# Reordered low parts on VectorE and GpSimd, and two weight loads moved from the first attention pairs to pairs 5 and 6

## The chip, the cores and the metric

The kernel runs on one core of a Trainium2 chip. The metric is the device time of one execution in microseconds; the time before is the median of three runs.

## The reference, cut to what matters

Causal attention over 2 batches of 12 heads (448 rows, head size 64), then a gated layer, then a second layer with a softmax-weighted unit and a layer norm:

```python
scores = scale * q @ k.T; masked; attn = exp(scores - max) / (sum + 1e-9)
x = (attn @ v), heads side by side            # 896 x 768
g = sigmoid(x @ w_gate) * (x @ w_val)         # 896 x 1536
x = g @ w_out                                 # 896 x 768
h = x @ w_in                                  # 896 x 1024
solu = h * softmax(h); ln = layer_norm(solu) * g_ln
out = ln @ w_out2                             # 896 x 768
```

All of it is float32. Every float32 operand of a product is split into a high part (rounded to the tensor engine's fast float32 form) and a low part (the rest), and a product is three products: high by high, high by low, low by high.

## The kernel before, in words

Attention works on 12 pairs of heads. Its order is written out by hand: a list `STEPS` of entries (offset, engine, function, first pair, last pair), in which entry (o, e, f) issues `f(p)` at step `s = 8 * p + o` on engine `e`. A pair has 8 steps. At each step the main loop goes through the engines (E tensor engine, A ScalarE, D VectorE, S the SyncE queue, P GpSimd), and within one engine through the list from top to bottom, so that the list's order decides between entries of one step. Each engine works its instructions off in the order in which they were issued. "Pair 7" below is the stretch in which the tensor engine starts with the score products of pair 7.

For a pair p the work is:

- `load_qk(p)` and `load_v(p)`, loads on SyncE's queue into two raw buffers each, so that a load for p + 2 must be issued after the last reading of p's buffer.
- `prep_k_hi`, `prep_q_hi`, `prep_v_hi` (L225, L236): the high parts, on GpSimd. `prep_k_lo` (L231, tile `qks`) and `prep_v_lo` (L231, tile `v`, two instructions): the low parts, on GpSimd; `prep_q_lo` (L252): q's low part, on VectorE. `prep_k_lo` also issues the load of q and k for p + 2, `prep_v_lo` that of v.
- `sc_mm`: masks (L352) and score products (L365) in two groups of tiles, (3, 0) and (2, 1). In a tile the third of three terms reads q's low part. `sc_max` (L380): row maxima on VectorE. `sc_exp` (L392): exponentials with their row sums, on ScalarE.
- `sums` (L396, GpSimd), `recips` (L400 and L401, VectorE): the reciprocals of the row sums. `rs_rows` (L406) writes them to DRAM in four small transfers, and `rs_bcast` (L412) reads them back spread over the partitions, after the small ones have landed.
- `tr_mm` (L435): transposes of the exponentials, in four units 0 to 3 that share two PSUM buffers. `tr_hi` (L442, ScalarE) copies a unit out as its high part, `tr_lo` (L231, VectorE, tile `pt`) takes its low part and so frees the buffer: unit 2 needs the low part of unit 0, unit 3 that of unit 1.
- `pv_mm` (L466): the product with v, in eight pieces. `x_mul` (L472, VectorE): the product by the reciprocals. `x_hi` (L223, ScalarE) and `x_lo` (L231, GpSimd, tile `xy`): the split of x.

In the order before, VectorE does in pair p: maxima of tiles 3 and 0, low part of unit 3 of pair p - 2, `prep_q_lo(p + 1)`, `recips(p - 1)`, maxima of tile 2, low part of unit 0 of pair p - 1, maxima of tile 1, low part of unit 1, `x_mul(p - 2)`, low part of unit 2. GpSimd does: `sums(p - 1)`, `prep_v_lo(p - 1)`, `x_lo(p - 3)`, `prep_k_lo(p + 1)`, `prep_k_hi(p + 2)`, `prep_q_hi(p + 2)`, `prep_v_hi(p)`.

The weights of the gated layer come as raw 64-bit words in chunks of 128 x 1536 words of 4 bytes, into two raw buffers. `dma_next()` issues the next load. In attention two are issued at fixed steps (8 and 12, both among the steps of pair 1); `bits_steps` turns a chunk into float32 from step 88 on, on ScalarE and VectorE, and issues the load that follows. A first part of the gated layer (`early_tiles`, L498) runs on the tensor engine behind step 96.

Of the kernel before, what the change touches and what calls it, by code (L numbers as in the profile page):

```python
# [19 lines left out]
B, H, S, D = 2, 12, 448, 64  # L20
# [18 lines left out]
def f32(ap):  # L39
    return ap.bitcast(F32)  # L40
# [3 lines left out]
def attn_moe_moe2(ctx: ExitStack, tc: tile.TileContext, qk, v, w_gv, w_out, w_in2, w_out2, g_ln, out):  # L44
# [50 lines left out]
    def dma_next():  # L95
        if pos["dma"] < len(order):
            it = order[pos["dma"]]
            a, n = src[it]
            raw = ring.tile([128, 2 * CH], I32, tag="raw", name="raw")
            nc.sync.dma_start(out=raw[:, :2 * n], in_=a.bitcast(I32))  # L100
            raw_t[it] = raw
            pos["dma"] += 1

    def bits_steps(it):


        assert order[pos["bits"]] == it
        pos["bits"] += 1
        n = src[it][1]
        w = raw_t.pop(it)[:, :2 * n].rearrange("p (n t) -> p n t", t=2)  # L110
        w0, w1 = w[:, :, 0], w[:, :, 1]
        nc.scalar.activation(out=w1.bitcast(F32), in_=w1.bitcast(F32), func=AF.Copy, scale=2.0 ** -112)  # L112
        yield
        tt = ring.tile([128, CH], I32, tag="t", name="t")[:, :n]
        nc.vector.tensor_scalar(out=tt, in0=w1, scalar1=3, scalar2=None, op0=ALU.logical_shift_left)  # L115
        yield
        nc.vector.scalar_tensor_tensor(out=tt, in0=w1, scalar=-2 ** 31, in1=tt,  # L117
                                       op0=ALU.bitwise_and, op1=ALU.bitwise_or)
        yield
        nc.vector.scalar_tensor_tensor(out=tt, in0=w0, scalar=29, in1=tt,  # L120
                                       op0=ALU.logical_shift_right, op1=ALU.bitwise_or)
        t_t[it] = tt.bitcast(F32)
        dma_next()
        yield
# [11 lines left out]
    def chunk_hi(c):  # L136
        if c < NCH and c not in hl_t:
            hl_t[c] = ring.tile([128, 2, CH], FR, tag="hl", name="hl")
            w_hi(c, hl_t[c][:, 0])

    def chunk_lo(c):
        if c in t_t:
            w_lo(c, hl_t[c][:, 0], hl_t[c][:, 1])
# [50 lines left out]
    with ExitStack() as actx:  # L194
# [14 lines left out]
        def load_qk(p):  # L209
            if p < NH // 2:  # L210
                r = qkr.tile([128, 2, S], F32, tag="qkr", name="qkr")
                both = qk[2 * p:2 * p + 2].rearrange("a d i s -> (a d) i s")
                for i in (1, 0) if p == 0 else (slice(0, 2),):
                    nc.sync.dma_start(out=r[:, i], in_=both[:, i])
                qk_raw[p] = r
# [14 lines left out]
        def sub(eng, out, a, b):  # L230
            (nc.gpsimd if eng == 'P' else nc.vector).tensor_tensor(out=out, in0=a, in1=b, op=ALU.subtract)  # L231
# [12 lines left out]

        def prep_k_lo(p):
            sub('P' if p else 'D', qk_sp[p][:, 3], qk_raw[p][:, 1], f32(qk_sp[p][:, 0]))
            if p:
                load_qk(p + 2)

        def prep_q_lo(p):  # L250
            t = qk_sp[p]
            nc.vector.scalar_tensor_tensor(out=t[:, 2], in0=qk_raw[p][:, 0], scalar=0.125, in1=f32(t[:, 1]),  # L252
                                           op0=ALU.mult, op1=ALU.subtract)

        def v_parts(p):
            return (v_raw[p % 2][:, 0:3].rearrange("p j (a d) -> p j a d", a=2),
                    *(v2[p % 2][:, i].rearrange("p j (a d) -> p j a d", a=3)[:, :, 0:3:2] for i in range(2)))
# [65 lines left out]
        prep_k_hi(0, 'D')  # L323
        prep_q_hi(0, 'A')
        prep_k_lo(0)
        prep_q_lo(0)
        load_qk(2)
        load_v(0)
# [49 lines left out]
        def sc_max(p, *tiles):  # L378
            for i in tiles:
                nc.vector.reduce_max(out=sum_t[p % 3][:, 8 + 2 * i:10 + 2 * i], in_=ps_both[p, i], axis=AX.X,  # L380
                                     negate=True)
# [47 lines left out]
        def tr_width(u):  # L429
            return 512 if u else S  # L430
# [13 lines left out]
        def tr_lo(p, u):  # L444
            w = tr_width(u)
            sub('D', pt_t[p][:, 1, u, :w], ps_tr.pop((p, u))[:, :w], f32(pt_t[p][:, 0, u, :w]))
# [39 lines left out]
        def early_tiles():  # L486
# [19 lines left out]
        NPR = NH // 2  # L506
# [13 lines left out]
            (14, 'A', lambda p: tr_hi(p, 2)), (6, 'A', lambda p: sc_exp(p, (1,)), 1),  # L520
            (-1, 'D', lambda p: sc_max(p, 3, 0), 2, 3),
            (0, 'D', lambda p: sc_max(p, 3, 0), 3), (16, 'D', lambda p: tr_lo(p, 3)),
            (-7, 'D', prep_q_lo, 3), (9, 'D', recips),
            (2, 'D', lambda p: sc_max(p, 2), 2), (11, 'D', lambda p: tr_lo(p, 0), 1), (3, 'D', lambda p: sc_max(p, 1), 2),
            (13, 'D', lambda p: tr_lo(p, 1)), (21, 'D', x_mul), (15, 'D', lambda p: tr_lo(p, 2)),
            (8, 'P', sums, 1), (9, 'P', prep_v_lo, 1), (25, 'P', x_lo, 0, NPR - 1), (23, 'P', x_lo, NPR - 1),
            (9, 'S', rs_rows), (9, 'S', rs_bcast),
            (-10, 'P', prep_k_hi, 3), (-9, 'P', prep_q_hi, 3), (-4, 'P', prep_k_lo, 3), (7, 'P', prep_v_hi, 1),
        )

        sc_mm(0, (0, 1))
        keep_warm(ps[:, 0], 6)
        prep_k_hi(1)
        prep_q_hi(1, 'A')
        prep_q_lo(1)
        prep_k_lo(1)
        for e in range(2):
            sc_max_of(0, e, 3, 0)
# [26 lines left out]
        def steps(s, eng):  # L565
            for s0, e, f, *ps in STEPS:
                p, r = divmod(s - s0, PER)
                lo, hi = (*ps, NPR)[:2] if ps else (0, NPR)
                if e == eng and r == 0 and max(lo, 1 if s0 < 0 else 0) <= p < hi:
                    f(p)  # L570


        for s in range(PER * NPR + 26):
            steps(s, 'E')
            for _ in range(2):
                if s >= PER * NPR and left and next(early):
                    left -= 1
            steps(s, 'A')
            steps(s, 'D')
            steps(s, 'S')  # L580
            steps(s, 'P')
            if s in (8, 12):
                dma_next()

            for c in range(2 * NE + 2):
                e = s - 88 - 8 * c
                if e in (3, 5, 7):
                    next(bits_now)
                if e == 8 and c < 2 * NE:
                    chunk_hi(c)  # L590
                if e == 9 and c < 2 * NE:
                    chunk_lo(c)
                if e == 0:
                    bits_now = bits_steps(c)
                    next(bits_now)
# [237 lines left out]
```

## Time and profile before

| what | value |
|---|---|
| median of three runs | 496.69 us (496.26 to 498.13) |
| the profiled execution | 497.59 us, span 495.8 us |
| tensor engine busy | 481.9 us (97%) |
| VectorE busy | 329.7 us (67%) |
| ScalarE busy | 221.8 us (45%) |
| GpSimd busy | 120.8 us (24%) |
| tensor engine clock | granted in full throughout |

A span runs from the first to the last instruction; the profiled execution's own time is 1.79 us longer. Shares of busy time are averages over stages: attention takes the first quarter, and there all five engines are busy most of the time. The trace names an instruction by its line, its engine, and the tile that it writes and reads; in brackets stand the idle time of its engine before it and what ended it. "x4" is four instructions shown as one row.

### The profile page before, as it was taken

How to read it: one execution, taken by the hardware profiler on the slowest of the kernel's cores; microseconds unless marked ns; L12 is line 12 of the kernel's file. 1: busy time of each engine (PE TensorE's matmuls, PEld its weight loads, DVE VectorE, ACT ScalarE, POOL GpSimd, SP SyncE). 2: the span in 40 equal slices, each digit the busy share in tenths (PEclk: the TensorE clock that was granted, in tenths of full speed). 3: DMA queues.
4: the chain of work that ended last, by engine and by line, in shares of the span. 5: the costliest groups of instructions: out<-in, count | busy, mean ns of one | idle time of the engine just before them, and what ended most of it. 6: DMA issues, size and time to landing. Idle time of an engine off the chain costs nothing.

```text
span 495.8 us, 7596 instructions
## 1 busy us (share of the span) xinstructions
PE 481.9 (97%) x2907; PEld 440.8 (89%) x2907; DVE 329.7 (67%) x508; ACT 221.8 (45%) x471; POOL 120.8 (24%) x190
## 2 busy tenths in 40 slices
PE   8979988999999999999999999999999999999997
PEld 7868878899999999999999999999988888899996
DVE  7788888887556788777779647777635887821110
ACT  6868787955334434534543423433421433323111
POOL 5749878530000000000000000000060778610000
PEclk9999999999999999999999999999999999999999
DMA  5454433243322535433444333533431221001001
GB/s 192 138 156 148 155 93 104 61 147 127 129 76 94 169 131 167 153 117 116 167 159 139 127 108 127 167 128 116 163 128 26 103 69 60 0 33 62 34 32 65
DMA packets 15685, 55.60 MB, mean 112 GB/s; under 512 B 2720, under 2 KB 4768, under 8 KB 15648
## 3 DMA queue, kind: packets, MB, share of 16 engines
q1 hardware_dynamic: 15648, 55.11, 33.1%
q8 instruction: 23, 0.38, 0.3%
q14 instruction: 14, 0.11, 0.1%
HBM read 52.30 MB, written 2.80 MB: 111 GB/s over the span
## 4 chain that ended last, share of the span: by engine, by line
PE 84%; DVE 7%; DMA 4%; issue 2%; ACT 1%; SPq 1%; DVEq 0%; ACTq 0%
PE gv L639 34%; PE pm L669 18%; PE po L762 12%; PE h L701 12%; DVE pt L231 2%; PE x L466 2%; DVE sum L380 2%; PE t L435 2%; PE gv L498 2%; DVE qks L252 2%; PE s L365 1%; DMA rd<-rs32q 1%; DMA rb<-rd 1%; PE tp L744 1%; DMA qkr<-in_qk_dram 1%
## 5 line engine op out<-in xcount | busy, mean ns | idle before, releaser
L639 PE MATMUL gv<-xy,hl 128*128 128x448 f32 x828 | 168.1, 365 | 0.0
L639 PEld LDWEIGHTS gv<-xy,hl 128*128 128x128 f32 x828 | 155.4, 188 | 12.3
L669 PE MATMUL pm<-g,hl 128*128 128x448 f32 x432 | 87.7, 365 | 0.0
L669 PEld LDWEIGHTS pm<-g,hl 128*128 128x128 f32 x432 | 81.1, 188 | 6.4
L686 POOL TENSOR_SCALAR t<-t,g_sb 128x768 f32<-128x768 f32 x8 | 9.0, 1124 | 247.7 <-PE pm L669 247.7
L134 DVE TENSOR_TENSOR hl<-t,hl 128x768 fp32r<-128x768 f32 x36 | 35.1, 975 | 40.8 <-ACT hl L131 39.1
L762 PE MATMUL po<-wo,lt 128*128 128x384 f32 x336 | 60.7, 340 | 0.0
L701 PE MATMUL h<-wi,xy 128*128 128x512 f32 x252 | 59.3, 396 | 0.0
L762 PEld LDWEIGHTS po<-wo,lt 128*128 128x128 f32 x336 | 58.7, 188 | 0.2 <-POOL wo L691 0.2
L701 PEld LDWEIGHTS h<-wi,xy 128*128 128x128 f32 x252 | 47.1, 187 | 11.4
L117 DVE SCALAR_TENSOR_TENSOR t<-raw,t 128x768 int32<-128x768 int32 (+1 forms) x56 | 52.6, 939 | 1.8
L120 DVE SCALAR_TENSOR_TENSOR t<-raw,t 128x768 int32<-128x768 int32 (+1 forms) x56 | 52.0, 929 | 1.7
L112 ACT ACTIVATE raw<-raw 128x768 f32<-128x768 f32 (+1 forms) x56 | 48.2, 867 | 9.2 <-DMA raw<-in_wo_dram 5.9
L466 PE MATMUL x<-pt,v 128*128 128x384 f32 (+3 forms) x252 | 51.0, 324 | 0.0
L392 ACT ACTIVATE p<-s,sum 128x320 f32<-128x320 f32 (+3 forms) x92 | 43.7, 494 | 14.4 <-DVE sum L380 11.1
L466 PEld LDWEIGHTS x<-pt,v 128*128 128x128 f32 x252 | 37.0, 190 | 1.6
L231 DVE TENSOR_TENSOR pt<-t,pt 128x512 fp32r<-128x512 f32 (+1 forms) x48 | 32.0, 666 | 4.7 <-ACT pt L442 4.6
L171 DVE TENSOR_TENSOR lt<-tp,lt 128x512 fp32r<-128x512 f32 x14 | 9.7, 690 | 36.4 <-ACT lt L170 36.4
L435 PE MATMUL t<-ident,p 128*128 128x128 f32 x180 | 28.0, 276 | 5.6 <-DVE pt L231 5.6
L115 DVE TENSOR_SCALAR t<-raw 128x768 int32<-128x768 int32 (+1 forms) x56 | 30.6, 546 | 2.7 <-ACT raw L112 2.7
L380 DVE TENSOR_REDUCE sum<-s 128x2 f32<-128x640 f32 (+3 forms) x44 | 28.8, 677 | 5.1 <-PE s L365 5.1
L131 ACT CAST hl<-t 128x768 fp32r<-128x768 f32 x36 | 30.0, 834 | 4.6 <-PE pm L669 4.2
(97 smaller groups left out, 481.6 us busy)
## 6 DMA issues: line engine op xcount, KB each, us to landing
raw<-in_gv_dram SPq DMA_DIRECT2D x24, 768.0 KB
raw<-in_wo_dram SPq DMA_DIRECT2D x20, 768.0 KB
raw<-in_wi_dram SPq DMA_DIRECT2D x12, 512.0 KB
qkr<-in_qk_dram SPq DMA_DIRECT2D x11, 448.0 KB
vr<-in_v_dram SPq DMA_DIRECT2D x12, 256.0 KB
rb<-rd SPq DMA_DIRECT2D x24, 112.0 KB
out_dram<-o SPq DMA_DIRECT2D x6, 384.0 KB
rd<-rs32q SPq DMA_DIRECT2D x48, 1.0 KB
```

Source lines behind the costliest of these rows:

```text
L112: nc.scalar.activation(out=w1.bitcast(F32), in_=w1.bitcast(F32), func=AF.Copy, scale=2.0 ** -112)
L117: nc.vector.scalar_tensor_tensor(out=tt, in0=w1, scalar=-2 ** 31, in1=tt, op0=ALU.bitwise_and, op1=ALU.bitwise_or)
L120: nc.vector.scalar_tensor_tensor(out=tt, in0=w0, scalar=29, in1=tt, op0=ALU.logical_shift_right, op1=ALU.bitwise_or)
L231: (nc.gpsimd if eng == 'P' else nc.vector).tensor_tensor(out=out, in0=a, in1=b, op=ALU.subtract)
L380: nc.vector.reduce_max(out=sum_t[p % 3][:, 8 + 2 * i:10 + 2 * i], in_=ps_both[p, i], axis=AX.X, negate=True)
L392: nc.scalar.activation(out=p_t[p % 2][:, POFF[i] + (1 - e) * n:POFF[i] + (2 - e) * n], in_=ps_sc[p, i][1 - e], func=AF.Exp, bias=mx, scale ...
L435: nc.tensor.transpose(ps[:, max(c, 0):max(c, 0) + 128], p_t[p % 2][:, k:k + 128], ident if c >= 0 else identx)
L466: nc.tensor.matmul(out=ps[:, q0:], lhsT=l, rhs=pt_t[pr][:, c, u, c0:c0 + S - q0], start=(chunk == 0 and n == 0), stop=(chunk == 7 and n == ...
L639: nc.tensor.matmul(out=ps[i, b], lhsT=w[:, a, cs], rhs=xy[kk][:, x, b * S:(b + 1) * S], start=(kk == 0 and a == 0 and x == 0), stop=(kk == ...
L669: nc.tensor.matmul(out=ps[b], lhsT=w[:, a, cs], rhs=g_t[kk][:, x, b * S:(b + 1) * S], start=(kk == 0 and a == 0 and x == 0), stop=(kk == N ...
L701: nc.tensor.matmul(out=h[:, n * 512:(n + 1) * 512], lhsT=xy[kk][:, a, tk], rhs=wi[n * NK + kk][:, c], start=(kk == 0 and i == 0), stop=(kk ...
L762: nc.tensor.matmul(out=ps[n], lhsT=lts[k // 4][:, a, k % 4], rhs=wo[k][:, c, cs], start=(k == 0 and i == 0), stop=(k == NF2 - 1 and i == 2))
```

## The change

In VectorE's list `recips` (9) now stands first, then the low part of unit 0 (offset 11 becomes 10), then the maxima of tiles 2 and 1. `prep_q_lo` goes from offset -7 to -2, behind `x_mul` (21, which falls on an earlier step of the pair) and ahead of the low part of unit 2 in the pair's order. `prep_v_lo` goes from offset 9 to 8 and stands ahead of `sums`. For pairs from 3 on, the load of q and k for p + 2 is issued by `prep_q_lo`, which is now the last reader of the raw buffer, and not by `prep_k_lo`. The two first weight loads are issued at steps 44 and 52.

```diff
         def prep_k_lo(p):
             sub('P' if p else 'D', qk_sp[p][:, 3], qk_raw[p][:, 1], f32(qk_sp[p][:, 0]))
-            if p:
+            if 0 < p < 3:
                 load_qk(p + 2)
 
         def prep_q_lo(p):
             t = qk_sp[p]
             nc.vector.scalar_tensor_tensor(out=t[:, 2], in0=qk_raw[p][:, 0], scalar=0.125, in1=f32(t[:, 1]),
                                            op0=ALU.mult, op1=ALU.subtract)
+            if p > 2:
+                load_qk(p + 2)
...
-            (-7, 'D', prep_q_lo, 3), (9, 'D', recips),
-            (2, 'D', lambda p: sc_max(p, 2), 2), (11, 'D', lambda p: tr_lo(p, 0), 1), (3, 'D', lambda p: sc_max(p, 1), 2),
-            (13, 'D', lambda p: tr_lo(p, 1)), (21, 'D', x_mul), (15, 'D', lambda p: tr_lo(p, 2)),
-            (8, 'P', sums, 1), (9, 'P', prep_v_lo, 1), (25, 'P', x_lo, 0, NPR - 1), (23, 'P', x_lo, NPR - 1),
+            (9, 'D', recips), (10, 'D', lambda p: tr_lo(p, 0), 1),
+            (2, 'D', lambda p: sc_max(p, 2), 2), (3, 'D', lambda p: sc_max(p, 1), 2),
+            (13, 'D', lambda p: tr_lo(p, 1)), (21, 'D', x_mul), (-2, 'D', prep_q_lo, 3), (15, 'D', lambda p: tr_lo(p, 2)),
+            (8, 'P', prep_v_lo, 1), (8, 'P', sums, 1), (25, 'P', x_lo, 0, NPR - 1), (23, 'P', x_lo, NPR - 1),
...
-            if s in (8, 12):
+            if s in (44, 52):
                 dma_next()
```

## Rows read from the trace of the kernel before

**Rows 1.** Stretches by pair (3, 4, 7, 11): length; busy time of each engine, clock, DMA.

```profile
23.16:33.81 10.65, 7.67 (x76) 6.62 (x76) 7.35 (x14) 6.17 (x22) 3.90 (x5) 1.00 0.58 178
33.81:41.29 7.48, 7.29 (x76) 6.62 (x75) 6.26 (x13) 6.20 (x22) 6.07 (x9) 1.00 0.42 134
57.21:65.16 7.95, 7.29 (x76) 6.62 (x76) 6.73 (x13) 6.21 (x22) 6.12 (x9) 1.00 0.36 123
...
88.97:97.28 8.31, 7.61 (x79) 6.99 (x78) 7.63 (x15) 8.09 (x28) 4.29 (x8) 1.00 0.28 86
```

**Rows 2.** Waits of PE, pairs 5 to 10: total us, times, longest.

```profile
PE t L435 <- DVE pt L231: 3.9, 6, 0.7
```

**Rows 3.** Instructions in order of time, pair 7: start, us, engine, line, tiles.

```profile
57.31 1.10 PE L365 MATMUL s<-qks 64*128 64x448 f32 x12
...
57.99 0.25 POOL L396 TENSOR_SCALAR rs8i<-sum 128x8 f32<-128x8 f32 x1 [1.62 <-ACT p L392]
...
58.32 1.42 POOL L231 TENSOR_TENSOR v<-vr,v 128x384 fp32r<-128x384 f32 x2
...
59.70 1.16 POOL L231 TENSOR_TENSOR xy<-xf,xy 128x448 fp32r<-128x448 f32 x1
...
60.26 1.08 DVE L252 SCALAR_TENSOR_TENSOR qks<-qkr,qks 128x448 fp32r<-128x448 f32 x1
...
60.49 0.53 ACT L442 CAST pt<-t 128x448 fp32r<-128x448 f32 x1
...
61.27 0.19 DVE L400 RECIPROCAL rs32t<-rs8i 128x8 f32<-128x8 f32 x1
...
61.63 0.78 DVE L380 TENSOR_REDUCE sum<-s 128x2 f32<-128x640 f32 x1
...
62.10 0.61 ACT L442 CAST pt<-t 128x512 fp32r<-128x512 f32 x1
62.33 0.62 DVE L231 TENSOR_TENSOR pt<-t,pt 128x448 fp32r<-128x448 f32 x1
62.51 0.56 POOL L225 TENSOR_SCALAR qks<-qkr 128x448 fp32r<-128x448 f32 x1
...
63.00 0.66 PE L435 MATMUL t<-ident,p 128*128 128x128 f32 x4 [0.66 <-DVE pt L231]
...
63.32 0.68 DVE L231 TENSOR_TENSOR pt<-t,pt 128x512 fp32r<-128x512 f32 x1
...
63.56 0.77 POOL L225 TENSOR_SCALAR v<-vr 128x384 fp32r<-128x384 f32 x2
...
64.28 0.60 PE L435 MATMUL t<-ident,p 128*128 128x128 f32 x4
...
65.08 0.69 DVE L231 TENSOR_TENSOR pt<-t,pt 128x512 fp32r<-128x512 f32 x1 [0.54 <-ACT pt L442]
```

**Rows 4.** Instructions in order of time, from pair 2 to pair 3.

```profile
14.17 0.42 SPq L100 DMA_DIRECT2D raw<-in_gv_dram  x1
...
25.97 0.62 DVE L472 TENSOR_TENSOR xf<-x,rb 128x448 f32<-128x448 f32 x1 [4.17 <-DMA rb<-rd]
```

**Rows 5.** Chain that ended last, to 135 us: start, length, what.

```profile
15.92 5.36 DMA rd<-rs32q
...
86.53 1.17 DMA rd<-rs32q
```

**Rows 6.** Instructions in order of time, pair 11 and the first one behind it.

```profile
93.95 0.60 PE L435 MATMUL t<-ident,p 128*128 128x128 f32 x4
...
97.28 0.33 PE L435 MATMUL t<-identx,p 128*128 128x128 f32 x1 [0.71 <-DVE pt L231]
```

**Rows 7.** Instructions on the split q and k: shortest, median, longest in ns.

```profile
L252 DVE SCALAR_TENSOR_TENSOR qks<-qkr,qks x12: 617/1075/1222, 4.6 to 84.1; 128x448 fp32r<-128x448 f32 x12
```

**Rows 8.** Instructions in order of time, pair 9: a load and its reader.

```profile
73.82 0.38 SPq L214 DMA_DIRECT2D qkr<-in_qk_dram  x1
...
79.16 0.57 POOL L225 TENSOR_SCALAR qks<-qkr 128x448 fp32r<-128x448 f32 x1 [0.93 <-DMA qkr<-in_qk_dram]
```

## The prediction

> **What bounds the kernel now.** I read the stretches first, one per head pair of the attention stage, then who waited for whom on the tensor engine, then one pair in order of time, then the two places where pairs differ. The tensor engine's clock is granted in full in every stretch shown [rows 1], so times differ by waits alone. From pair 5 to pair 10 a pair takes 7.95 us, of which the tensor engine is busy 7.29; pair 4 takes 7.48 and pair 3 takes 10.65 with 7.67 busy [rows 1]. (A pair's stretch runs from its masks to the next pair's; the row of pair 7, 57.21 to 65.16, stands for six between 7.93 and 7.97.) After attention the tensor engine runs without such waits, so what attention saves should reach the end.
>
> In pairs 5 to 10 the engine has one kind of wait: six times the transposes of line 435 wait for a low part of line 231, 3.9 us together [rows 2]. The reader is to follow one of them backwards [rows 3]. The transposes of unit 2 at 63.00 stood 0.66 us still, until the vector engine had finished the low part of unit 0 (62.33 + 0.62 = 62.95), which frees their PSUM buffer. That low part needed only ScalarE's copy of unit 0, over at 60.49 + 0.53 = 61.02. It started 1.3 us later because q's low part (60.26, 1.08 us), the reciprocals (61.27) and the third tile's maxima (61.63) stand ahead of it in VectorE's order. So the bound is the order on VectorE.
>
> Pair 3 has another cause [rows 4, 5]. The first weight load is issued at 14.17, just ahead of the four small transfers of the first pair's reciprocals. Those land 5.36 us after the last is issued, where the same transfers take 1.17 us late in the stage [rows 5]. The broadcast, the product that reads it, and all that is queued behind the product on VectorE follow: the product waits 4.17 us, until 25.97 [rows 4]; over pair 3 the tensor engine is idle 10.65 - 7.67 = 2.98 us [rows 1].
>
> **The change, part by part. First, the order on VectorE (pairs 5 to 10).** Taking q's low part out lets the reciprocals start at 60.26; they and the transpose take 61.63 - 61.27 = 0.36, so VectorE is free at 60.62. The low part of unit 0, now next, waits for ScalarE until 61.02, runs from about 61.05 to 61.67, and unit 2's transposes, ready at 63.00 - 0.66 = 62.34, no longer wait [rows 3]. The maxima start at 61.67 rather than 61.63, so nothing is late there. The low part of unit 1 comes 0.70 (61.63 to 62.33, the maxima) and 0.99 (62.33 to 63.32) after 61.05, at 62.74; ScalarE's copy of unit 1 is over at 62.71; it ends at 63.42. Unit 3's transposes, then due at 64.28 - 0.66 = 63.62, have 0.2 us to spare: that edge is next.
>
> What a pair saves is bounded from below by the wait itself, 3.9 us over six pairs [rows 2], and from above by pair 11, which has no q part to prepare and the old order otherwise: there unit 2's transposes start 93.95 - 88.97 = 4.98 us into the pair, against 63.00 - 57.21 = 5.79, which is 0.81 [rows 1, 3, 6]. Six pairs: 3.9 to 4.9. I take 0.75 each, nearer to pair 11, since that is this very pipeline without the wait: **4.5 us**. A pair is then 7.2 us.
>
> q's low part itself goes behind the product, where VectorE stood idle 0.54 us before 65.08, waiting for ScalarE [rows 3]. By the shift above (63.32 to 62.74) the product is over at 65.08 - 0.54 - 0.58 = 63.96; q's low part runs to 64.58 at its shortest form (0.62) or 65.04 at its usual (1.08) [rows 7]. The next pair starts at 64.41 and its third term, which reads it, comes about half way through the twelve dots of 1.10 us that start 0.10 into a pair [rows 3]: about 65.0. Covered, with 0 to 0.4 us; I cost it at nothing, and if the cover is gone it is rival 1.
>
> **Second, v's low part ahead of the sums.** GpSimd stood idle 1.62 us ahead of the sums, waiting for ScalarE's exponentials [rows 3]. v's high part is over at 63.56 + 0.77 = 64.33; the low part of 1.42 us fits to 65.75, before the 57.99 + 7.95 = 65.94 at which the next sums ran before. With the shorter pair the sums may come some 0.4 us late, but the reciprocals that wait for them are due 3.05 us into the pair (60.26 - 57.21), at 67.46: 1.4 us of cover. Cost nothing. Behind the reciprocals on VectorE are the low part of unit 0, the maxima and so the tensor engine; a late sums would stall all of it.
>
> **Third, the loads of q and k behind q's low part.** The load of two pairs ahead is now issued at about 64.6 to 65.05, 7.4 to 7.8 into a pair; on SP's queue it stays behind the reciprocal transfers but now goes ahead of v's load. The slowest landing seen took 79.16 - 73.82 = 5.3 us [rows 8], so it lands by 12.7 to 13.1, that is 5.5 to 5.9 into the next pair. From there GpSimd needs 1.05 (62.51 to 63.56), 0.77, 1.42 and 0.25 for both high parts, v and the sums, 3.5 together [rows 3, 7]: 9.0 to 9.4, against reciprocals due at 7.2 + 3.05 = 10.25. Cost nothing, 0.8 us to spare.
>
> **Fourth, the two weight loads.** In pair 3 the delay of 5.36 - 1.17 = 4.19 us was made by all that was in flight: by their shapes 768 KB of weights, 448 of q and k, 256 of v. By size, the weights' share is 4.19 x 768/1472 = 2.2 us. The small transfers then land at about 19, and the broadcast before or about 21.8 (25.97 - 4.17), when the product is due; a rest of a microsecond on VectorE is harmless, since of 4.17 us only 2.98 reached the tensor engine. Pair 3 saves at least its idle time, 2.98, and at most 10.65 - 7.2 = 3.45 if it runs like the rest: **3.2 us**. Pair 4: 7.48 - 7.2, **0.3 us**.
>
> In pairs 5 and 6 the loads come back on SP's queue ahead of the load of q and k for pairs 8 and 9, which lands 2.2 us later: 7.7 to 8.1, and the sums at 11.2 to 11.6 instead of the due 10.25. Of this 1.0 to 1.4 us, 0.4 is the time in which the low part of unit 0 waits for ScalarE anyway, and 0.6 is unit 2's spare time (62.34 against 61.67). So nothing at a quicker landing, and up to 1.0 us for each load, the second of which starts from a later queue. I take 0.35 each: **-0.7 us** (0 to -2.0). The weights themselves are first used in pair 11, so their own lateness costs nothing.
>
> **Fifth, pair 11 and the end.** There q's low part was absent already, so the new order only adds VectorE's 0.4 us wait for ScalarE's copy (60.62 to 61.02 in the same place of pair 7), and VectorE sets the pace: the transposes at 97.28 waited 0.71 us for it [rows 6]. Also v's low part now meets other instructions of the weights' preparation. **-0.5 us** (0 to -1.3, that is 0.4 and two delays of 1.08 - 0.62).
>
> Sum: 4.5 + 3.2 + 0.3 - 0.7 - 0.5 = 6.8 us. The profiled execution took 497.59 us (span 495.8 and 1.79 around it), so it would be 490.8; it was 0.90 above the median of 496.69, which becomes **489.9 us**.
>
> **Rivals.** *1. q's low part meets v's low part on the way.* Now q's low part begins at 60.26 while GpSimd's x part runs to 59.70 + 1.16 = 60.86, and it ends at 61.34, 0.48 behind that; alone it takes 0.62 [rows 3, 7]. In the new order v's low part follows v's high part directly and lies in the very place of q's low part. If it is locked out until the first of v's two instructions is over (three quarters of the 1.42 by their columns, so 64.33 + 1.07) it ends 0.48 behind that, at 65.9, 0.9 after the third term is due; since either may come first I count half, 0.4 in each pair: 6 x 0.4 = 2.4 off, 492.3 us. For it: the places agree to half a microsecond. Against: GpSimd also gets rid of its collision now, and a late q part has its own spare time. Chance 0.14. The Trainium skill's "SBUF — State Buffer" (Who interferes with whom) has this as a rule: a VectorE instruction with two SBUF inputs and a GpSimd instruction that reads SBUF exclude each other, and the later one to issue is blocked until the first is over. By that rule, which the 0.48 us bears out, the sum is 6.8 where the two miss each other and 4.4 where they meet.
>
> *2. The loads in pairs 5 and 6 disturb more than their own pair:* late q and k carry GpSimd's lateness through pairs 7 to 9, 3.5 us instead of 0.7: 492.7 us. For: pair 3 shows what a load ahead of small transfers does. Against: a pair has a spare microsecond or more on GpSimd. Chance 0.10.
>
> *3. The first stall stays:* the small transfers wait behind q, k and v instead, and pair 3 saves 1.0 and not 3.2: 492.1 us. For: 704 of 1472 KB remain in flight. Against: the weights are the larger half, and the product has 1.2 us of lateness (4.17 - 2.98) that never reached the tensor engine. Chance 0.08.
>
> *4. Slower: the sums, behind v's low part, behind a late load, hold the reciprocals in every pair.* To be 3 us slower, 9.8 us have to be lost over pairs 3 to 10, 1.2 each, and 0.4 us of slack first: the reciprocals 1.6 late, which with 0.8 to spare takes a landing of 5.3 + 0.8 + 1.6 = 7.7 us after issue in each pair. That gives 499.7 us. For: the load is issued behind a later instruction and everything hangs on one queue. Against: the slowest landing seen is 5.3 us. Chance 0.04.
>
> **How the numbers follow.** The forecast has 0.60, with its own range of 488.4 to 491.6 (savings of 8.3 to 5.1, the bounds not all at one end); the rivals 0.36; 0.04 is left for several together that cancel the gain. The range reaches down to 488.0 and up to 492.9, which takes in rivals 1 to 3. A change of 0.5%, 2.5 us, is about what a measurement of this kernel can tell from none: faster than 494.2 is the forecast and the rivals 1 to 3, 0.92; the same 0.04; slower 0.04.
>
> **What would show it.** Right: no idle time ahead of unit 2's transposes in pairs 5 to 10; a pair of about 7.2 us; the product of pair 0 without its 4.17 us wait; pair 3 below 7.8 us. Unit 0's low part starts straight after ScalarE's copy. Wrong: dots waiting for q's low part (rival 1); GpSimd waiting over 2 us for q and k in pairs 6 and 7, and reciprocals waiting for the sums (2, 4); a product that still waits for its broadcast (3); unit 3's transposes waiting for unit 1's low part, the edge with 0.2 us.

## The result, and the profile after

The changed kernel takes 491.68 us (median of 8 runs, 490.61 to 495.26) against 496.70 us before (8 runs): a ratio of 0.9906, 95% interval 0.9879 to 0.9933. The profiled execution took 492.44 us with a span of 490.7 us, 5.1 us under the span before. The forecast was 489.9 us, the range 488.0 to 492.9.

The stretches by pair of the changed kernel, for pairs 3, 6, 7, 8 and 11, with the columns of [rows 1] (length; busy PE, PEld, DVE, ACT, POOL; clock; DMA share; GB/s):

```profile
23.02:30.24 7.22, 7.22 (x76) 6.52 (x75) 6.50 (x13) 5.38 (x19) 3.30 (x5) 1.00 0.40 133
...
44.76:51.99 7.23, 7.23 (x76) 6.52 (x75) 6.43 (x13) 6.19 (x23) 4.75 (x7) 1.00 0.69 241
51.99:59.88 7.89, 7.51 (x76) 6.55 (x75) 6.35 (x13) 6.19 (x23) 5.74 (x9) 1.00 0.63 187
59.88:68.94 9.06, 7.52 (x76) 6.54 (x77) 6.37 (x13) 6.21 (x23) 7.17 (x12) 1.00 0.43 140
...
83.42:92.19 8.77, 7.63 (x79) 6.93 (x79) 8.14 (x16) 8.53 (x29) 5.69 (x8) 1.00 0.18 56
```

Pair 3 went from 10.65 to 7.22 us, and quiet pairs (5, 6, 9 and 10, in which nothing waits for a late transfer) from 7.95 to 7.24: in them the tensor engine is busy for the whole stretch. Pairs 7 and 8 are the exceptions. The two weight loads stand at steps of pairs 5 and 6, but the queue comes to them at 45.36 and 54.66, in the stretches of pairs 6 and 7 (0.69 of the DMA engines' time in pair 6): the loss shows one pair behind each. Pair 11 grew from 8.31 to 8.77.

How a quiet pair now runs is seen on VectorE and on the tensor engine's weight loads (PEld), in order of time, for the places that answer to [rows 3] and [rows 4]:

```profile
22.15 0.62 DVE L474 TENSOR_TENSOR xf<-x,rb 128x448 f32<-128x448 f32 x1 [0.67 <-DMA rb<-rd]
...
48.58 0.62 DVE L231 TENSOR_TENSOR pt<-t,pt 128x448 fp32r<-128x448 f32 x1 [0.34 <-ACT pt L444]
49.12 1.28 DVE L382 TENSOR_REDUCE sum<-s 128x2 f32<-128x640 f32 x2
...
50.32 0.68 DVE L231 TENSOR_TENSOR pt<-t,pt 128x512 fp32r<-128x512 f32 x1
...
51.05 0.42 PEld L437 LDWEIGHTS t<-ident,p 128*128 128x128 f32 x4 [0.29 <-DVE pt L231]
...
51.45 0.62 DVE L252 SCALAR_TENSOR_TENSOR qks<-qkr,qks 128x448 fp32r<-128x448 f32 x1
52.07 0.69 DVE L231 TENSOR_TENSOR pt<-t,pt 128x512 fp32r<-128x512 f32 x1
```

The product of pair 0 waits 0.67 us for its broadcast and not 4.17. The low part of unit 0 waits 0.34 us for ScalarE's copy and then starts, as forecast; q's low part fills the gap ahead of unit 2's low part and takes its shortest form. Unit 1's low part is over at 51.00, and the weight loads of unit 3's transposes had already waited 0.29 us for it: that edge has nothing to spare, though the matmuls in flight cover the wait.

What goes wrong in pairs 7 and 8 is one chain over four engines. In order of time, with the SyncE queue as SPq:

```profile
45.36 1.20 SPq L100 DMA_DIRECT2D raw<-in_gv_dram  x1
46.67 0.36 SPq L214 DMA_DIRECT2D qkr<-in_qk_dram  x1
...
48.27 1.30 SPq L408 DMA_DIRECT2D rd<-rs32q  x4
...
52.55 0.56 POOL L225 TENSOR_SCALAR qks<-qkr 128x448 fp32r<-128x448 f32 x1 [2.87 <-DMA qkr<-in_qk_dram]
53.43 1.19 SPq L414 DMA_DIRECT2D rb<-rd  x2
54.66 0.59 SPq L100 DMA_DIRECT2D raw<-in_gv_dram  x1
55.36 0.36 SPq L214 DMA_DIRECT2D qkr<-in_qk_dram  x1
...
55.86 0.26 POOL L398 TENSOR_SCALAR rs8i<-sum 128x8 f32<-128x8 f32 x1
56.15 0.20 DVE L402 RECIPROCAL rs32t<-rs8i 128x8 f32<-128x8 f32 x1 [1.01 <-POOL rs8i L398]
...
58.95 0.66 PE L437 MATMUL t<-ident,p 128*128 128x128 f32 x4 [0.35 <-DVE pt L231]
...
61.60 0.57 POOL L225 TENSOR_SCALAR qks<-qkr 128x448 fp32r<-128x448 f32 x1 [3.15 <-DMA qkr<-in_qk_dram]
...
65.19 0.20 DVE L402 RECIPROCAL rs32t<-rs8i 128x8 f32<-128x8 f32 x1 [2.17 <-POOL rs8i L398]
...
66.20 0.66 PE L437 MATMUL t<-ident,p 128*128 128x128 f32 x4 [1.19 <-DVE pt L231]
```

The weights stand ahead of q and k on the queue; the first instruction that reads q or k starts 5.9 us after their issue (46.67 to 52.55), GpSimd stands still 2.87 us and comes late to v and the sums; the reciprocals wait 1.01 us for the sums, and the transposes for the low parts behind the reciprocals. The second time is worse, for the broadcast of the pair before had to wait for its small transfers (48.27 to 53.43), which kept the second weight load and all that follows it back on the queue.

### The profile page after: what moved, and what is told of

Same layout as the page of the kernel before. It is cut to its first block, busy times and chain, and to the rows that moved or that the text cites. A ratio compares the mean times of both kernels' runs of the same rounds, so it can differ in the third digit from the quotient of the medians.

```text
span 490.7 us, 7583 instructions
## 1 busy us (share of the span) xinstructions
PE 481.4 (98%) x2907; PEld 439.8 (90%) x2907; DVE 327.5 (67%) x508; ACT 221.2 (45%) x471; POOL 119.9 (24%) x190
## 4 chain that ended last, share of the span: by engine, by line
PE 90%; DVE 4%; ACT 3%; DMA 2%; issue 0%; SPq 0%; POOL 0%; ACTq 0%
PE gv L641 34%; PE pm L671 18%; PE po L764 12%; PE h L703 12%; PE x L468 5%; PE t L437 3%; PE s L367 3%; DVE sum L382 2%; PE gv L500 2%; ACT p L394 2%; PE tp L746 1%; DVE pt L231 1%; DMA qkr<-in_qk_dram 1%; PE s L354 0%; DMA rb<-rd 0%
## 5 line engine op out<-in xcount | busy, mean ns | idle before, releaser
L183 ACT ACTIVATE wk<-gv 128x448 f32<-128x448 f32 x23 | 11.3, 542 | 44.3 <-PE gv L641 44.3
```

## The experiments

The first seven are profiles of one execution each; numbers 8 to 11 were also timed over several runs. The length of a pair is the distance between the first masks of two pairs in each trace; pair 11 is counted to the first transposes behind it.

| kernel | span | pairs 3 to 10, us | pair 11 |
|---|---|---|---|
| before | 495.8 | 10.65 7.48 7.97 7.95 7.95 7.94 7.93 7.94 | 8.31 |
| changed | 490.7 | 7.22 7.28 7.24 7.23 7.89 9.06 7.23 7.25 | 8.77 |
| 1 weights late | 488.7 | 7.24 7.24 7.26 7.23 7.73 7.27 7.25 7.39 | 8.78 |
| 2 weights behind q and k | 489.9 | 7.25 7.23 7.25 7.25 7.34 7.23 7.97 7.75 | 9.10 |
| 3 weights early | 495.0 | 13.35 7.25 7.23 7.44 7.47 7.23 7.49 7.24 | 8.76 |
| 4 sums first | 490.1 | 7.24 7.26 7.27 7.24 7.24 8.17 7.25 7.26 | 8.77 |
| 5 weights alone | 493.4 | 7.82 7.94 7.96 7.94 7.94 7.49 8.85 7.49 | 8.31 |
| 6 maxima first | 489.4 | 7.21 7.52 7.20 7.63 7.21 7.94 7.21 7.22 | 8.78 |
| 7 q early | 496.4 | 8.24 8.27 8.26 8.28 8.26 8.26 8.29 8.26 | 8.77 |
| 8 late, and pair 11 | 489.1 | 7.25 7.55 7.26 7.40 7.50 7.25 7.24 7.24 | 8.74 |
| 9 sums first, late | 487.8 | 7.24 7.26 7.24 7.24 7.23 7.24 7.25 7.25 | 8.30 |
| 10 q and weights alone | 487.6 | 7.21 7.22 7.23 7.20 7.21 7.22 7.22 7.20 | 8.32 |
| 11 changed again | 490.1 | 7.24 7.72 7.25 7.23 7.25 8.73 7.26 7.25 | 8.77 |

**1. The weight loads behind all loads of q and k.**

```diff
-            if s in (44, 52):
+            if s in (74, 82):
```

> The two first weight loads go to steps 74 and 82, behind the last load of q and k (step 70) and ahead of their first use at step 88; all else as changed. Theory (the weight loads stand ahead of the loads of q and k on SyncE's queue and make them, GpSimd, the sums and the reciprocals late): pairs 7 and 8 fall from 7.89 and 9.06 us to about 7.24 each, the reciprocals no longer wait for the sums there, the span falls from 490.7 to about 488.3. Rival (the load of q and k is late because it is now issued behind q's low part, whatever stands ahead of it): pairs 7 and 8 stay near 7.9 and 9.1, span 490.7.

The span fell to 488.7 us, pair 8 to 7.27, and the reciprocals wait for the sums nowhere. The theory holds for the weights, but pair 7 stayed at 7.73 (and pair 10 at 7.39, with q's low part at 1.12 us), and for another reason. GpSimd, VectorE and the tensor engine in order of time:

```profile
51.24 1.80 POOL L231 TENSOR_TENSOR v<-vr,v 128x384 fp32r<-128x384 f32 x2
51.29 1.44 DVE L252 SCALAR_TENSOR_TENSOR qks<-qkr,qks 128x448 fp32r<-128x448 f32 x1
...
52.79 0.73 PE L367 MATMUL s<-qks 64*128 64x448 f32 x8 [0.21 <-DVE qks L252]
```

v's low part began 0.05 us ahead of q's low part, which took 1.44 us instead of 0.62, and the score products waited for it. This is rival 1. At that place in the changed kernel's profile the two did not meet: while q's low part ran (51.45 to 52.07), GpSimd stood still for q and k.

**2. The same weight loads two steps later, behind the load of q and k of the same pair.**

```diff
-            if s in (44, 52):
+            if s in (46, 54):
```

> The two weight loads stay in pairs 5 and 6 but two steps later (46 and 54), so that they stand behind the load of q and k of the same pair on SyncE's queue; the same bytes in the same pairs. Theory (order on the queue): q and k land on time, pairs 7 and 8 at 7.24 to 7.5, span 488.3 to 489. Rival (bytes: any 768 KB more in these pairs make the transfers late): pairs 7 and 8 stay over 7.8 and over 8.8, span 490.5.

Pairs 7 and 8 were nearly quiet (7.34 and 7.23), as the order on the queue would have it. Yet pairs 9 and 10 took 7.97 and 7.75, which neither side had expected; and the span, 489.9, lies outside the theory's 488.3 to 489. The queue and VectorE in order of time:

```profile
48.30 1.30 SPq L408 DMA_DIRECT2D rd<-rs32q  x4
52.38 1.09 SPq L414 DMA_DIRECT2D rb<-rd  x2
...
55.64 1.31 SPq L408 DMA_DIRECT2D rd<-rs32q  x4
61.53 1.09 SPq L414 DMA_DIRECT2D rb<-rd  x2
62.73 0.53 SPq L214 DMA_DIRECT2D qkr<-in_qk_dram  x1
...
70.83 0.20 DVE L402 RECIPROCAL rs32t<-rs8i 128x8 f32<-128x8 f32 x1 [1.09 <-POOL rs8i L398]
```

The weights no longer stand ahead of the load of q and k, but still, as in the changed kernel, ahead of the small transfers. The broadcast is issued 4.1 and 5.9 us after them, against 2.3 to 3.7 in undisturbed pairs of the changed kernel (41.10 to 44.23, for one), and the next load of q and k stands behind the broadcast; the reciprocals then wait for the sums, 1.09 us in pair 9 and 0.87 in pair 10. So the bytes do disturb, two pairs later than in the changed kernel, by way of the queue's wait.

**3. The weight loads at their old steps, with the reorderings.**

```diff
-            if s in (44, 52):
+            if s in (8, 12):
```

> The weight loads back at steps 8 and 12; the three reorderings stay. Theory: the product of pair 0 waits about 4 us for its broadcast again, pair 3 takes 10 to 10.6 us, pairs 7 and 8 7.24 each: span 490.7 - 2.46 + 3 = 491.2. Rival (the reordering, not the weight loads, took the stall out of pair 3): pair 3 stays at 7.2, span 488.3.

The stall of pair 3 is back and larger than before the change: 13.35 us. The span, 495.0, is 3.8 us above what was expected. VectorE and the tensor engine in order of time:

```profile
25.80 0.62 DVE L474 TENSOR_TENSOR xf<-x,rb 128x448 f32<-128x448 f32 x1 [4.28 <-DMA rb<-rd]
26.34 0.61 DVE L252 SCALAR_TENSOR_TENSOR qks<-qkr,qks 128x448 fp32r<-128x448 f32 x1
...
27.01 1.22 PE L367 MATMUL s<-qks 64*128 64x448 f32 x8 [3.21 <-DVE qks L252]
```

The product waits as in [rows 4], but now q's low part is queued behind it, and the score products of pair 3 wait 3.21 us for that. That is about half of the 6.1 us by which the pair exceeds a quiet one. The rest is the tensor engine's clock, in the stretch behind the wait (columns as in [rows 1]):

```profile
27.01:32.70 5.69, 5.69 (x40) 5.48 (x40) 3.07 (x7) 1.62 (x5) 2.23 (x2) 0.50 0.44 145
```

The granted clock is the lower of the two levels there (0.50, 1.2 GHz) and full again from 33.30; the engine is busy throughout, and 5.69 us at half the clock are an estimated 2.8 us lost. In the kernel before the longest wait in pair 3 was 1.45 us, and the clock stayed full [rows 1]. Behind the product, q's low part has no cover for a product that waits: without the move of the weights the reorderings save 0.8 us of span in all, in this one execution. Pairs 6, 7 and 9 took 7.44 to 7.49, behind q parts of 1.18 to 1.20 us, as in experiment 1.

**4. The sums ahead of v's low part again.**

```diff
-            (8, 'P', prep_v_lo, 1), (8, 'P', sums, 1),
+            (8, 'P', sums, 1), (8, 'P', prep_v_lo, 1),
```

> The sums ahead of v's low part on GpSimd again, all else as changed. Theory (a late load of q and k holds GpSimd, and v's low part adds its 1.42 us between that and the sums): the reciprocals' waits of 1.01 and 2.17 us in pairs 7 and 8 shrink by 1.4 each to 0 and 0.75, pairs 7 and 8 take about 7.25 and 7.7, the others 7.24, span 488.7. Rival (the order of sums and v's low part makes no difference, since the load alone decides): span 490.7. A third: v's low part behind the sums meets q's low part and costs 0.3 us in every pair, span 491.

Pair 7 was quiet and pair 8 took 8.17, with one wait of the reciprocals of 1.30 us left (0.75 expected). The quiet pairs stayed at 7.24 to 7.27. The span was 490.1 and not 488.7: behind pair 11 the weights' preparation came 0.75 us later, since there v's low part met it (the instruction of line 120 took 1.70 us instead of 0.95). So v's low part ahead of the sums costs in pairs 7 and 8 and saves at the end.

**5. The weight loads alone, in the kernel before.**

```diff
-            if s in (8, 12):
+            if s in (44, 52):
```

> The kernel before with the weight loads alone moved to steps 44 and 52. In its old order they stand behind the load of q and k, which is issued in step 44 by k's low part. Theory: pair 3 falls from 10.65 to about 7.95 (the old order's pace), pairs 5 to 10 stay at 7.95, span 495.8 - 2.8 = 493.0, no wait of the reciprocals for the sums. Rival (the weights in pairs 5 and 6 disturb the pairs behind them in any order): pairs 7 and 8 grow by 0.6 and 1.8 as in the changed kernel, span 495.4.

Pair 3 fell to 7.82, the old order's pace, so the weights had made the stall of pair 3. But pair 9 took 8.85: the product there waited 1.43 us for its broadcast. The place in pairs 5 and 6 disturbs in the old order too, in another pair. It costs nothing in sum, however: pairs 8 and 10 took 7.49 and not 7.94. In both, q's low part took 0.61 us instead of 1.07, and the transposes waited under 0.2 us. In pair 8 it began just ahead of v's low part, and that one became longer instead (1.85 us, not 1.42):

```profile
65.79 0.61 DVE L252 SCALAR_TENSOR_TENSOR qks<-qkr,qks 128x448 fp32r<-128x448 f32 x1
65.84 1.85 POOL L231 TENSOR_TENSOR v<-vr,v 128x384 fp32r<-128x384 f32 x2
```

The same holds for pair 4 of the kernel before, which took 7.48:

```profile
36.86 0.62 DVE L252 SCALAR_TENSOR_TENSOR qks<-qkr,qks 128x448 fp32r<-128x448 f32 x1
36.96 1.79 POOL L231 TENSOR_TENSOR v<-vr,v 128x384 fp32r<-128x384 f32 x2
```

The span of 493.4 lies near the theory's 493.0 and away from the rival's 495.4.

**6. The third tile's maxima ahead of unit 0's low part again.**

```diff
-            (9, 'D', recips), (10, 'D', lambda p: tr_lo(p, 0), 1),
-            (2, 'D', lambda p: sc_max(p, 2), 2), (3, 'D', lambda p: sc_max(p, 1), 2),
+            (9, 'D', recips),
+            (2, 'D', lambda p: sc_max(p, 2), 2), (11, 'D', lambda p: tr_lo(p, 0), 1), (3, 'D', lambda p: sc_max(p, 1), 2),
```

> The third tile's maxima ahead of the first unit's low part again (offsets 2 and 11), q's low part stays behind the product, all else as changed. Theory (q's low part was the whole of the wait, and the low part of unit 0 has to wait for ScalarE's copy in any case, so its move is worth nothing in pairs 5 to 10 and costs 0.4 us in pair 11): quiet pairs stay at 7.24, pair 11 falls from 8.77 to 8.3, span 490.2. Rival (both moves are needed, as the forecast has them together): quiet pairs grow by 0.2 to 0.5, span 492.

Quiet pairs take 7.20 to 7.22: unit 0's move is worth nothing there once q's low part is gone. Pairs 4 and 6 were longer, the tensor engine's score products being stretched as where q's low part meets v's; pair 8 waited for the sums. Pair 11 did not fall (8.78). Its traces, here and in the changed kernel, show two different causes. In the changed kernel unit 3's transposes wait 0.43 us for unit 1's low part (0.42 in experiment 4), behind the low part of unit 0 that waits for ScalarE's copy; the kernel before has no such wait:

```profile
90.19 0.66 PE L437 MATMUL t<-ident,p 128*128 128x128 f32 x4 [0.43 <-DVE pt L231]
```

In this experiment that wait is gone. But v's low part (88.47, 2.14 us) meets the weights' preparation, whose instruction takes 1.38 us instead of 0.95, and the transposes that end the pair wait 1.15 us instead of 0.71:

```profile
88.91 1.38 DVE L117 SCALAR_TENSOR_TENSOR t<-raw,t 128x768 int32<-128x768 int32 x1
...
90.95 0.33 PE L437 MATMUL t<-identx,p 128*128 128x128 f32 x1 [1.15 <-DVE pt L231]
```

**7. q's low part in its old place, the other edits kept.** The load of q and k is again issued by `prep_k_lo`.

```diff
-            (9, 'D', recips), (10, 'D', lambda p: tr_lo(p, 0), 1),
+            (-7, 'D', prep_q_lo, 3), (9, 'D', recips), (10, 'D', lambda p: tr_lo(p, 0), 1),
...
-            (13, 'D', lambda p: tr_lo(p, 1)), (21, 'D', x_mul), (-2, 'D', prep_q_lo, 3), (15, 'D', lambda p: tr_lo(p, 2)),
+            (13, 'D', lambda p: tr_lo(p, 1)), (21, 'D', x_mul), (15, 'D', lambda p: tr_lo(p, 2)),
```

> q's low part in its old place ahead of the reciprocals, and the load of q and k with k's low part as before; the low part of unit 0 ahead of the maxima, sums behind v's low part, weight loads at steps 44 and 52. Theory: unit 2's transposes no longer wait, but unit 1's low part comes at 63.3 of the old pair 7 and unit 3's transposes wait some 0.4 us for it, so a pair takes about 7.6; the load of q and k stands ahead of the weights, so pairs 7 and 8 are like the others. Span 490.7 - 2.5 + 8 x 0.4 = 491.4. Rival (the move of unit 0 alone was enough): pairs of 7.24, span 488.3.

A pair took 8.26 us, more than before the change, where 7.6 was expected. In order of time:

```profile
57.97 1.14 POOL L231 TENSOR_TENSOR xy<-xf,xy 128x448 fp32r<-128x448 f32 x1 [0.69 <-ACT xy L223]
...
59.07 1.14 POOL L231 TENSOR_TENSOR qks<-qkr,qks 128x448 fp32r<-128x448 f32 x1
59.12 1.57 DVE L252 SCALAR_TENSOR_TENSOR qks<-qkr,qks 128x448 fp32r<-128x448 f32 x1
...
61.61 0.66 PE L435 MATMUL t<-ident,p 128*128 128x128 f32 x4 [0.42 <-DVE pt L231]
...
63.40 0.66 PE L435 MATMUL t<-ident,p 128*128 128x128 f32 x4 [0.34 <-DVE pt L231]
```

With v's low part out of the way GpSimd comes to x and to k's low part earlier, and q's low part, begun 0.05 us behind k's, takes 1.57 us. Both units wait then. As the order in this trace suggests, the move of v's low part, costed at nothing, makes the old place of q's low part worse; no run moves v's low part alone.

**8. The weight loads late, and in pair 11 the old order on VectorE.**

```diff
-            (9, 'D', recips), (10, 'D', lambda p: tr_lo(p, 0), 1),
-            (2, 'D', lambda p: sc_max(p, 2), 2), (3, 'D', lambda p: sc_max(p, 1), 2),
+            (9, 'D', recips), (10, 'D', lambda p: tr_lo(p, 0), 1, NPR - 2),
+            (2, 'D', lambda p: sc_max(p, 2), 2), (11, 'D', lambda p: tr_lo(p, 0), NPR - 2), (3, 'D', lambda p: sc_max(p, 1), 2),
...
-            if s in (44, 52):
+            if s in (74, 82):
```

> The weight loads at steps 74 and 82, and for the last two pairs the low part of unit 0 behind the maxima as before (so in pair 11's stretch VectorE does not wait for ScalarE); all else as changed. Theory: pairs 7 and 8 at 7.24 and pair 11 0.4 us shorter: span 487.9, about 2.8 us or 0.6% under the changed kernel. Rival (pair 11's 0.46 us come from v's low part meeting the weights' preparation, not from the wait): span 488.3.

490.61 us, 0.9876 of before (0.9846 to 0.9906). Pair 11 stayed at 8.74 and pairs 4, 6 and 7 took 7.40 to 7.55, with q's low part at 1.28, 1.14 and 1.23 us in the stretches that end with their start. The span of 489.1 lies above both forecasts; the rival was right for pair 11.

**9. The same with the sums ahead of v's low part.**

```diff
-            (8, 'P', prep_v_lo, 1), (8, 'P', sums, 1),
+            (8, 'P', sums, 1), (8, 'P', prep_v_lo, 1),
```

> The changed kernel with the weight loads at steps 74 and 82, the sums ahead of v's low part again, and for the last two pairs the low part of unit 0 behind the maxima. Theory (with the weights out of the way GpSimd runs early, so that v's low part meets q's low part in some pairs, which made pairs of 7.4 to 7.7 us in the two runs before; with the sums first v's low part lies a microsecond later and misses it; and pair 11 has the old order on both engines): all pairs from 3 to 10 at 7.20 to 7.30, no q part longer than 0.8 us, pair 11 at 8.3, span 487.4. Rival (q's low part is lengthened by other GpSimd instructions whichever comes first): pairs of 7.5 remain, span 488.7.

489.68 us (five runs, 489.61 to 489.80), 0.9841 of before (0.9813 to 0.9869). All eight pairs lie between 7.23 and 7.26, and no q part in them is longer than 0.80 us. Pair 11 is at 8.30: it needs the old order on both engines, since either new one alone (4, and 6 and 8) gave 8.74 to 8.78.

**10. The kernel before with q's low part and the weight loads moved, and nothing else.** The load of q and k goes with q's low part, as in the change.

```diff
-            (-7, 'D', prep_q_lo, 3), (9, 'D', recips),
+            (9, 'D', recips),
...
-            (13, 'D', lambda p: tr_lo(p, 1)), (21, 'D', x_mul), (15, 'D', lambda p: tr_lo(p, 2)),
+            (13, 'D', lambda p: tr_lo(p, 1)), (21, 'D', x_mul), (-2, 'D', prep_q_lo, 3), (15, 'D', lambda p: tr_lo(p, 2)),
...
-            if s in (8, 12):
+            if s in (74, 82):
```

> The kernel before with two edits alone: q's low part (and the load of q and k with it) behind the product, and the weight loads at steps 74 and 82. The sums stay ahead of v's low part, the third tile's maxima ahead of the first unit's low part in every pair. Theory (these two carry the whole gain): pairs 3 to 10 at 7.20 to 7.30, pair 11 at 8.3, span 487.4 as in the run beside it. Rival (the other two reorderings are worth something in the quiet pairs): pairs of 7.4 to 7.6, span 489 to 490.

489.39 us (five runs, 489.24 to 489.62), 0.9835 of before (0.9811 to 0.9860): the quickest. Two of its stretches (pairs 5 and 11), and the line of q's low part with shortest, median and longest:

```profile
37.49:44.72 7.23, 7.23 (x76) 6.54 (x75) 6.40 (x14) 6.11 (x23) 6.53 (x11) 1.00 0.40 135
...
80.77:89.09 8.32, 7.62 (x79) 6.99 (x79) 7.71 (x16) 8.01 (x28) 4.32 (x8) 1.00 0.48 157
```

```profile
L252 DVE SCALAR_TENSOR_TENSOR qks<-qkr,qks x12: 615/662/1281, 4.6 to 80.2; 128x448 fp32r<-128x448 f32 x12
```

The tensor engine has no idle time left in the quiet pairs. Two edits carry the whole gain; the two reorderings left out add nothing to it. The weights stand later here than in the change (steps 74 and 82): what the two edits give with the weights at 44 and 52 was not run.

**11. The changed kernel beside them.**

> The changed kernel itself beside the two others on the same chip, for their difference: span 490.7, pairs 7 and 8 at 7.9 and 9.1, time about 2.5 to 3.3 us above the two others if the theory holds, and within 1 us of them if the rival does.

493.31 us (six runs, 491.64 to 494.82), 0.9912 of before (0.9884 to 0.9941), so 3.9 us above experiment 10 on the same chip. It also moves more from run to run (the two longest, 494.28 and 494.82, have a mean granted clock of 0.997, the other four 0.999 or 1.000), and its profile is not that of the first one: pair 4 took 7.72, pair 7 was quiet (7.25), and pair 8 took 8.73. GpSimd, VectorE and the tensor engine there:

```profile
29.65 1.81 POOL L231 TENSOR_TENSOR v<-vr,v 128x384 fp32r<-128x384 f32 x2
29.69 1.46 DVE L252 SCALAR_TENSOR_TENSOR qks<-qkr,qks 128x448 fp32r<-128x448 f32 x1
31.20 0.72 PE L367 MATMUL s<-qks 64*128 64x448 f32 x8 [0.22 <-DVE qks L252]
```

Rival 1 thus occurs in the changed kernel itself, in single pairs, when v's low part and q's come together.

## Why the prediction was right, and where it was off

*The order on VectorE, 4.5 us.* Right in kind: the six waits of [rows 2] are gone; the three that pairs 7 and 8 have instead come from the late sums. A quiet pair takes 7.24 where 7.2 was forecast; the six pairs 5 to 10 took 47.68 us before, so six quiet ones save 47.68 - 6 x 7.24 = 4.2 us. But the credit went to three instructions ahead of unit 0's low part, and experiments 6 and 10 show that q's low part alone was the obstacle. And most of that was not its place but its length: where it took 0.61 or 0.62 us in the old order (pair 4 before, pairs 8 and 10 of experiment 5), a pair took 7.48 or 7.49, so of the 0.71 us some 0.46 go with its 1.08 us, behind an instruction of GpSimd, and 0.25 with its place. That with unit 0 ahead of the maxima "nothing is late there" was right, and it is also nothing gained.

*Pair 3, 3.2 us, and pair 4, 0.3 us.* Measured 10.65 - 7.22 = 3.4 and 7.48 - 7.28 = 0.2. The small transfers were delayed by the weights, as experiments 3 and 5 show from both sides.

*The weight loads in pairs 5 and 6, -0.7 us.* **This is the term that was mis-sized.** Measured against quiet pairs it is (7.89 - 7.24) + (9.06 - 7.24) = 2.5 us. The step that failed is "I take 0.35 each". First, I counted 1.0 us of slack for late reciprocals, 0.4 by ScalarE's copy and 0.6 by unit 2; a wait of 1.01 us already cost pair 7 0.65, because the edge which I had named as next (unit 3 behind unit 1's low part, 0.2 us) is reached first: the transposes at 58.95 are unit 3's. That edge has no slack at all (51.05), so the slack is ScalarE's copy alone: in the changed kernel and experiments 2, 4 and 11, each wait of the reciprocals of 0.40 to 2.17 us costs its pair the wait less 0.35 to 0.38. The lateness itself, 1.0 to 1.4 us, was sized rightly for the first load. Second, I let both loads cost the same. The first one delays the small transfers, the broadcast that waits for them holds the queue, and the second weight load starts with that lateness in hand; its wait was 2.17 us, and the sum of 2.5 lies outside my bound of 2.0. That is rival 2's outcome at two thirds of its price, carried by the queue and not, as it has it, by GpSimd, which stood idle 3.15 us for q and k. Experiment 1 takes it away and brings pair 8 to 7.27, experiment 2 shifts it two pairs on.

*Pair 11 and the end, -0.5 us.* Measured 8.77 - 8.31 = 0.46. The size was right, and the cause in the changed kernel is the one named first, the wait for ScalarE's copy (0.43 us at 90.19, experiment 6). The second, v's low part meeting the weights' preparation, is also worth about 0.4, but only where the first is absent: each brings pair 11 to 8.74 to 8.78 by itself, and together no more.

*The sum.* 4.2 + 3.4 + 0.2 - 2.5 - 0.5 = 4.8 (4.95 by the unrounded lengths, 74.12 - 69.17), and 0.14 us with which pair 3 already starts earlier (23.16 and 23.02): the 5.1 us by which the span fell, where 6.8 was forecast. The median of 491.68 us lies 0.1 above the range that the forecast had for itself, 488.4 to 491.6; it is inside the stated range because that took in the rivals. On the other chip of experiment 11 the same kernel took 493.31, above the stated range, at nearly the same ratio to the kernel before.

*v's low part ahead of the sums, costed at nothing.* In the quiet pairs of the profiled execution that holds. It does not in general: it is what brings v's low part to the place of q's (experiments 1, 8 and 11, against 9), and what makes a late GpSimd later (without it, in experiment 4, the waits of 1.01 and 2.17 us fell to none and 1.30). Rival 1 was given 0.4 us in each of six pairs, 2.4 in all; it comes in some pairs and costs 0.1 to 0.5 us in each.

*q's low part behind the product, "covered".* True as long as the product itself does not wait. Experiment 3 shows what stands behind that cover: with a product that is 4.28 us late, the score products wait 3.21, and the tensor engine's clock falls on top of it.

*Rivals 3 and 4.* The product of pair 0 still waited 0.67 us, without a trace on the tensor engine. Rival 4's mechanism ran in two pairs, not in eight.

The Trainium skill's "SBUF — State Buffer" (Who interferes with whom) has a VectorE instruction with two SBUF inputs blocked until a GpSimd instruction that reads SBUF and was issued first is over. The runs agree: in experiment 7 q's low part, begun behind k's, ended at 60.69, 0.48 us behind the end of that at 60.21. For the queue, the Trainium skill's "DMA: Bandwidth & Descriptors" (Two DMAs through the same engine are not ordered) has the issuing engine wait for the first transfer's completion before it issues one that reads what the first wrote; of the 5.2 us between 48.27 and 53.43, 1.30 issue the small transfers, and the 3.9 left are that wait, with all later loads behind it.

## What to carry to other kernels

A load that nobody needs soon belongs where no transfer with a waiting reader is on the same queue or behind it; a place in a middle stage is not free when the queue also carries small transfers that wait for one another. When several reorderings come together, try the one that removes the wait alone: here two edits of the four, with the weights later still, gave more than all, with less spread. When an instruction stands in the way, look first whether it is long only because it begins behind another engine's. And where an instruction is moved behind another, ask what happens if that other one waits.

## What the runs showed of the hardware that was not expected

Two weight loads of 768 KB, issued in the stretches of pairs 6 and 7, show their cost one pair behind each in the changed kernel (pairs 7 and 8) and three pairs behind each in experiment 2 (pairs 9 and 10), passed on by the queue's in-order waits. A VectorE instruction that begins 0.04 or 0.05 us behind one of GpSimd's takes between 1.44 and 1.57 us instead of 0.62 (experiments 1, 7 and 11); one that begins 0.05 us ahead keeps its 0.61, and GpSimd's grows (experiment 5). So one kernel has pairs of 7.24 and of 7.7 us in different executions. And a tensor engine that stood still for 3.21 us in one piece went on at half the clock for at least 5.69 us, and the pair became 6.1 us longer (experiment 3).
